# K tiles of four batches, V tiles of two, and extra matmuls in three waits: a change to an attention and MLP decode kernel

## The chip, the cores and the metric

The kernel runs on one core of a Trainium2 chip. A core has TensorE (PE: matmuls, with its weight loads shown apart as PEld), VectorE (DVE), ScalarE (ACT), GpSimd (POOL) and SyncE (SP), and 16 DMA engines that move data between HBM and the on-chip SBUF. Matmuls write to PSUM; DVE and ACT bring results from there to SBUF. The metric is the device time of one execution in microseconds (us), lower is better. Timed without the profiler, the kernel before took 399.53 us (median of three runs, 399.5 to 399.78).

## The reference, cut to what matters

One decode step of a transformer block with adaptive layer norm: 8 batches, one token each, width 512. The attention has 32 query heads over 8 key/value heads (REP = 4), head width 128, and reads the last W = 2048 positions of a cache of 8192. All numbers are 32-bit floats.

```python
mod = (_silu(c) @ w_mod).reshape(c.shape[0], 6, 1, -1)
sa, ca, ga, sb, cb, gb = (mod[:, 0], ..., mod[:, 5])
h = _layernorm(x) * (1 + ca) + sa
# attention: q = h @ wq; k, v = the last W rows of the caches
scores = jnp.einsum("bhqd,bhkd->bhqk", q, k) * (Dh ** -0.5)
p = _softmax(scores, axis=-1)
o = jnp.einsum("bhqk,bhkd->bhqd", p, v)
x = x + ga * (o.reshape(B, Sq, Hq * Dh) @ wo)
h = _layernorm(x) * (1 + cb) + sb
x = x + gb * (relu(h @ w1 + b1) ** 2 @ w2 + b2)
```

The K and the V that are read make 64 MiB each: 8 batches x 8 heads x 2048 x 128 x 4 bytes, twice. The weights add some 30 MB.

## The kernel before, in words

**Tiles.** SBUF holds eight equal buffers, `slots` (L78), of 16 KB per partition, 2 MiB each. Every large load goes into one of them: a K tile (two batches of one key/value head: 64 partitions for each batch, every second partition, 32 positions of 128 numbers on each), a V tile (the same), half of a `wq` group, a `wo` part, parts of `w_mod`, `w1` and `w2`. K and V tiles are loaded by two DMAs of 1 MiB, one for each batch (L97-98).

**Order of the loads.** All of them are issued by SP in one fixed list, `loads` (L132-143): `modA`, two `wq` pieces, then step by step K tile s and V tile s-5, with `wo` parts between, and at the end `modB`, `modC`, the biases, `w1`, `w2`. `pump` (L146) issues the next entries as long as `free` has a buffer; `done` (L151) gives a buffer back when the instruction that last reads it has been written down. The list is strictly in order, so an entry that waits for its buffer holds up all behind it.

**Steps.** The loop at L445 runs 38 steps. N = 32 of them take one K tile each, four (C = 4) for each key/value head. In step s:

- `transposes(s, 0..3)` (L299): 32 PE transposes of 128x128, in eight groups of four into two PSUM buffers; ACT and DVE copy the groups in turn to `kT`. After the last group the K tile is done.
- `scores(s - 1)` (L312): eight products of the padded queries `qpad` with every second column of `kT`, summed into one PSUM tile `s_ps` for the whole head.
- once for each head the softmax in four pieces, `soft_a` to `soft_d` (L328 to L388): copy and maximum, the maximum per query, exponential and sum, transposed probabilities.
- `weighted(s - 5)` (L390): eight products of probabilities with a V tile and four DVE operations that pick the diagonal blocks; then the V tile is done.
- once for each head `gather` (L415) and `project_o` (L431).
- in step 5 `project_q(1)` (L268), which projects the queries of the second half of the heads and ends the use of the last `wq` pieces. `project_q(0)` runs before the loop.

**Tail.** After the loop (L475 on) come the modulation by `modB`, the second layer norm, `h @ w1` (L532: the first two of four row groups, then a wait for the second half of `w1`, then the other two), the DVE work that makes `rT` (L205, L542-544), the bias product (L548), `rT @ w2` in 14 groups of eight instructions (L553), two DVE operations (L561-562) and the store (L563). `w2` arrives in five DMAs: rows 0-4, 4-8, 8-12, 12 and 13 of its 14 groups.

Work between engines is ordered by semaphores; on each engine the instructions run in program order.

Of the kernel before, what the change touches and what calls it, by code (L numbers as in the profile page):

```python
# [14 lines left out]
SLOTS = 8  # L15
V_LAG = 5
PV_LAG = 5
# [3 lines left out]
def tile_adaln_cached_attention_mlp(  # L21
# [34 lines left out]
    ktp = ctx.enter_context(tc.tile_pool(name="ktp", bufs=6))  # L56
# [20 lines left out]

    slots = [consts.tile([P, NJ * DH], F32, name=f"slot{i}") for i in range(SLOTS)]  # L78
    free = list(range(SLOTS))
    held = {}  # L80
    r_kc = "(p kc) n -> p kc n"

    def load(key):
# [5 lines left out]
        s = free.pop(0)  # L89
        t = slots[s]  # L90
        held[key] = s
        if kind in "KV":

            src = k_cache if kind == "K" else v_cache
            hk, c = divmod(i, C)
            v = src[2 * c : 2 * c + 2, hk, SK - W :, :].rearrange("u (p j) d -> u p (j d)", p=H)
            for u in range(2):  # L97
                nc.sync.dma_start(t[u::2, :], v[u])
            return
# [6 lines left out]
        elif kind == "modB":  # L106
            v = w_mod[:, 2 * D : 5 * D].rearrange(r_kc, p=P)[:, 2 * i : 2 * i + 2]
# [5 lines left out]
        elif kind == "w1":  # L113
            v = w1.rearrange(r_kc, p=P)[:, 2 * i : 2 * i + 2]
        else:
            v = w2.rearrange("(p c) n -> p c n", p=P)
            for lo, hi in ((0, 4), (4, 8)) if i == 0 else ((8, 12), (12, 13), (13, 14)):
                o = lo - 8 * i
                n = hi - lo
                nc.sync.dma_start(  # L120
                    t[:, D * o : D * (o + n)].rearrange("p (c n) -> p c n", n=D), v[:, lo:hi, :]
                )
# [4 lines left out]
    def slot(key, n):  # L127

        t = slots[held[key]]
        return t[:, : t.shape[1] // n * n].rearrange("p (a n) -> p a n", n=n)  # L130

    loads = [("modA", 0), ("wq", 0), ("wq", 1)]  # L132
    for s in range(N + V_LAG):
        if s == V_LAG:
            loads += [("wq", 2), ("wq", 3)]
        if s < N:
            loads.append(("K", s))
        v = s - V_LAG
        if v >= 0:
# [3 lines left out]
    loads += [("modB", 0), ("modB", 1), ("modC", 0), ("b", 0), ("w1", 0), ("w1", 1), ("w2", 0), ("w2", 1)]  # L143
    at = [0]

    def pump():  # L146
        while at[0] < len(loads) and (free or loads[at[0]][0] == "b"):
# [3 lines left out]
    def done(*keys):  # L151
        for k in keys:
            free.append(held.pop(k))
# [20 lines left out]
    qpad = consts.tile([P, HKV, B, 32], F32, name="qpad")  # L174
    nc.gpsimd.memset(qpad, 0.0)
# [6 lines left out]
    nc.vector.tensor_reduce(uq, bq.rearrange("p (c u) -> p u c", u=2), axis=AX.X, op=ALU.add)  # L182

# [84 lines left out]
    def project_q(r):  # L268
# [13 lines left out]
        qs = work.tile([P, 512], F32, name="qs", tag="a")  # L282
# [4 lines left out]
        v = pT_.rearrange("p (t g b) -> p g b t", t=REP, g=4)  # L287
        for g in range(4):
            hk = 4 * r + g
            flat = qpad[:, hk].rearrange("p b m -> p (b m)")  # L290
            dest = bass.AP(tensor=flat.tensor, offset=flat.offset, ap=[flat.ap[0], [36, B], [1, REP]])
            nc.vector.tensor_copy(dest, v[:, g, :B, :])
# [6 lines left out]
    def transposes(n, g):  # L299

        k = slot(("K", n), DH)
        t = ktp.tile([P, 8, P], F32, name="kT")
        for a in range(2):
            p = ps_kt.tile([P, 4, P], F32, name="kt_ps")
            for i in range(4):
                nc.tensor.transpose(p[:, i, :], k[:, 8 * g + 4 * a + i, :], ident)  # L306
            (nc.vector.tensor_copy if a else nc.scalar.copy)(t[:, 4 * a : 4 * a + 4, :], p)  # L307
        KTS[n, g] = t
        if g == 3:
            done(("K", n))  # L310

    def scores(n):  # L312
        hk, c = divmod(n, C)
        if c == 0:
            s_ps[0] = ps_1.tile([P, 512], F32, name="s_ps")
        for u in range(2):
            for g in range(4):
                nc.tensor.matmul(  # L318
                    s_ps[0][32 * g : 32 * g + 32, :].rearrange("p (i r) -> p i r", i=8),
                    qpad[:, hk, 2 * c + u, :],  # L320
# [279 lines left out]
```

## Time and profile before

| | |
|---|---|
| time, median of three runs | 399.53 us (399.5 to 399.78) |
| time of the profiled execution | 399.68 us |
| its span, first to last instruction | 397.9 us |
| PE busy | 329.2 us (83%) |
| DVE, ACT busy | 177.1 us (45%), 94.9 us (24%) |
| bytes moved by DMA | 165.25 MB, 415 GB/s over the span |
| granted TensorE clock, mean | 0.979 |

The time of an execution is 1.8 us longer than the span between its first and last instruction. "Busy" counts the time in which an engine works on at least one instruction; PE at 83% is the busiest compute engine. The DMA row gives the mean load of the 16 DMA engines.

### The profile page before, as it was taken

Reading aid. Unit: us, or ns where it says so; the run is one execution under the profiler, and the core shown is the slowest. Engines: PE = TensorE matmul, PEld = TensorE weight load, DVE = VectorE, ACT = ScalarE, POOL = GpSimd, SP = SyncE. Lnnn points to the kernel's source line nnn. Section 1 sums busy time; section 2 is a strip of 40 time slices with the busy share of each in tenths; the row PEclk is TensorE's granted clock in tenths of the full one; section 3 lists DMA queues with packets and bytes.
Section 4 is the critical chain, followed back from the end, with each engine's and each line's share of the span. In section 5 each row is a group of like instructions: output and inputs, shape, how many; then the busy total and the mean of one; then the engine's idle time right before and its main releaser. Section 6 shows DMA issues by size and latency. Waiting matters only on the chain.

```text
span 397.9 us, 6384 instructions
## 1 busy us (share of the span) xinstructions
PE 329.2 (83%) x2632; PEld 168.1 (42%) x2632; DVE 177.1 (45%) x411; ACT 94.9 (24%) x169; POOL 3.3 (1%) x11
## 2 busy tenths in 40 slices
PE   0688889899999999998688899899789998765765
PEld 0245455344454445444344454455344544221124
DVE  6223345344564456445534554456245544542222
ACT  1223244122322322232122232232122312120010
POOL 3000000000000000000000000000000000000000
PEclk9999999999999999999999999999899999998897
DMA  8999999999999999999999999999999999999993
GB/s 308 433 428 423 418 434 423 427 429 418 428 430 428 428 418 432 428 422 425 432 425 427 428 430 424 427 420 430 423 432 425 430 423 431 423 423 417 419 413 128
DMA packets 15357, 165.25 MB, mean 415 GB/s; under 512 B 2392, under 2 KB 2656, under 8 KB 4448
## 3 DMA queue, kind: packets, MB, share of 16 engines
q1 hardware_dynamic: 15184, 164.71, 98.2%
q8 instruction: 21, 0.34, 0.4%
q10 hardware_dynamic: 144, 0.13, 0.1%
q14 instruction: 8, 0.07, 0.0%
HBM read 164.77 MB, written 0.07 MB: 414 GB/s over the span
## 4 chain that ended last, share of the span: by engine, by line
DMA 59%; PE 27%; DVE 8%; ACT 4%; issue 2%; ACTq 0%; DVEq 0%; SPq 0%
DMA slot<-in_A_v_cache_dram 21%; DMA slot<-in_A_k_cache_dram 20%; DMA slot<-in_A_wo_dram 11%; PE kt_ps L306 9%; PE s_ps L318 6%; DMA slot<-in_B_w_dram 5%; PE o_ps L398 4%; DVE kT L307 4%; PE m_ps L273 2%; DMA slot<-in_w_mod_dram 2%; ACT kT L307 2%; DVE o_sb L411 2%; PE m_ps L553 1%; PE m_ps L222 1%; PE m_ps L532 1%
## 5 line engine op out<-in xcount | busy, mean ns | idle before, releaser
L306 PE MATMUL kt_ps<-ident,slot 128*128 128x128 f32 x1024 | 149.2, 283 | 29.1 <-ACT kT L307 13.2
L306 PEld LDWEIGHTS kt_ps<-ident,slot 128*128 128x128 f32 x1024 | 109.6, 142 | 102.7 <-issue 58.2
L307 DVE COPY kT<-kt_ps 128x512 f32<-128x512 f32 x128 | 88.2, 689 | 99.5 <-PE kt_ps L306 86.6
L307 ACT COPY kT<-kt_ps 128x512 f32<-128x512 f32 x128 | 74.8, 584 | 205.6 <-PE kt_ps L306 195.8
L398 PE MATMUL o_ps<-slot,pT 128*32 128x512 f32 x512 | 64.0, 610 | 7.7 <-DMA slot<-in_A_v_cache_dram 6.2
L318 PE MATMUL s_ps<-kT,qpad 128*32 128x512 f32 x512 | 65.4, 627 | 0.0
L411 DVE SCALAR_TENSOR_TENSOR o_sb<-o_ps,diag,o_sb 128x128 f32<-128x128 f32 x96 | 33.7, 351 | 3.4
L409 DVE TENSOR_SCALAR o_sb<-o_ps,diag 128x128 f32<-128x128 f32 x32 | 11.2, 350 | 44.4 <-PE o_ps L398 44.4
L398 PEld LDWEIGHTS o_ps<-slot,pT 128*32 128x32 f32 x512 | 16.4, 110 | 32.7 <-issue 30.3
L318 PEld LDWEIGHTS s_ps<-kT,qpad 128*32 128x32 f32 x512 | 13.5, 109 | 27.2 <-issue 27.2
L222 PE MATMUL m_ps<-slot,cT 128*32 128x256 f32 (+2 forms) x96 | 8.3, 502 | 9.3 <-DMA slot<-in_w_mod_dram 9.3
L332 DVE TENSOR_REDUCE mx<-ss 128x1 f32<-128x512 f32 x8 | 5.5, 686 | 13.7 <-ACT ss L330 13.7
L420 PE MATMUL m_ps<-o_sb,pick 128*32 128x512 f32 x64 | 8.4, 594 | 3.1 <-DVE o_sb L411 1.7
L273 PE MATMUL m_ps<-slot,h1T 128*32 128x512 f32 x64 | 8.9, 703 | 2.0 <-DVE h1T L205 2.0
L378 DVE TENSOR_TENSOR pT<-m_ps,mine 128x512 f32<-128x512 f32 x16 | 10.2, 681 | 0.0
L435 PE MATMUL wo_ps<-slot,oT 128*32 128x512 f32 x64 | 9.3, 651 | 1.1 <-DVE oT L425 1.1
L424 DVE STREAM_TRANSPOSE tr<-m_ps 128x512 f32<-128x512 f32 x8 | 5.7, 716 | 9.5 <-PE m_ps L420 9.5
L222 PEld LDWEIGHTS m_ps<-slot,cT 128*32 128x32 f32 x96 | 3.7, 140 | 13.6 <-issue 13.6
L330 ACT COPY ss<-s_ps 128x512 f32<-128x512 f32 x8 | 4.7, 586 | 18.9 <-PE s_ps L318 18.9
L375 PE MATMUL m_ps<-ident,pr 128*128 128x128 f32 x64 | 8.6, 274 | 0.4 <-DVE pr L359 0.3
L358 ACT ACTIVATE pr<-ss,nm 128x512 f32<-128x512 f32 x8 | 6.2, 774 | 9.7 <-DVE nm L354 9.7
L375 PEld LDWEIGHTS m_ps<-ident,pr 128*128 128x128 f32 x64 | 7.2, 140 | 1.6 <-DVE pr L359 1.2
(114 smaller groups left out, 92.1 us busy)
## 6 DMA issues: line engine op xcount, KB each, us to landing
slot<-in_A_k_cache_dram SPq DMA_DIRECT2D x64, 1024.0 KB, 19.6
slot<-in_A_v_cache_dram SPq DMA_DIRECT2D x64, 1024.0 KB, 19.6
slot<-in_A_wq_dram SPq DMA_DIRECT2D x4, 2048.0 KB, 17.0
slot<-in_A_wo_dram SPq DMA_DIRECT2D x4, 2048.0 KB, 22.0
slot<-in_B_w_dram SPq DMA_DIRECT2D x2, 1792.0 KB, 19.8
slot<-in_w_mod_dram SPq DMA_DIRECT2D x2, 1536.0 KB, 21.4
slot<-in_B_w_dram SPq DMA_DIRECT2D x3, 1024.0 KB, 19.9
slot<-in_w_mod_dram SPq DMA_DIRECT2D x1, 2048.0 KB, 8.4
```

Of the source, the lines that this page charges most:

```text
L222: nc.tensor.matmul(pm[32 * q : 32 * q + 32, : nq * P].rearrange("p (m n) -> p m n", m=nq), cT[:, kc, :], wv[:, :, q, :], start=(kc == 0), ...
L273: nc.tensor.matmul(pq[32 * g : 32 * g + 32, :], hT[:, kc, :], w[:, kc % 2, 512 * g : 512 * g + 512], start=(kc == 0), stop=(kc == NQ - 1),)
L306: nc.tensor.transpose(p[:, i, :], k[:, 8 * g + 4 * a + i, :], ident)
L307: (nc.vector.tensor_copy if a else nc.scalar.copy)(t[:, 4 * a : 4 * a + 4, :], p)
L318: nc.tensor.matmul(s_ps[0][32 * g : 32 * g + 32, :].rearrange("p (i r) -> p i r", i=8), qpad[:, hk, 2 * c + u, :], KTS[n, g][:, :, u::2], ...
L375: nc.tensor.transpose(pp[:, i * P : (i + 1) * P], pr[:, 4 * a + i].rearrange("p r u -> p (r u)"), ident)
L378: nc.vector.tensor_mul(PT_[hk][:, a].rearrange("p x i r -> p i x r"), pp.rearrange("p (i x r) -> p i x r", i=4, r=2 * REP), mine.rearrange ...
L398: nc.tensor.matmul(o[32 * g : 32 * g + 32].rearrange("p j d -> p (j d)"), PT_[hk][:, h, C * g + c].rearrange("p i r -> p (i r)"), v[:, j : ...
L409: nc.vector.tensor_scalar(d, o[:, 0, :], diag[:, 0:1], None, op0=ALU.mult)
L411: nc.vector.scalar_tensor_tensor(d, o[:, j, :], diag[:, j : j + 1], d, op0=ALU.mult, op1=ALU.add)
L420: nc.tensor.matmul(pp[32 * t : 32 * t + 32, :], pick[:, t, :], o.rearrange("p c d -> p (c d)"), start=True, stop=True)
L435: nc.tensor.matmul(wo_ps[32 * i : 32 * i + 32, :], oT[hk % 2][:, i, :], w[:, 4 * (hk % 2) + i, :], start=(hk == 0), stop=(hk == HKV - 1),)
```

## The change

K and V get buffers of their own sizes. Two "big" buffers of 32 KB per partition hold K tiles of four batches (half of the batches of one head), loaded by one DMA of 4 MiB with 32 KB in one piece for each partition; partition 4p + u holds batch u's positions. They hold `modB` and `w1` later. Five "small" buffers of 16 KB hold V tiles (batches c and c + 4, one DMA of 2 MiB each), `wq`, `wo`, `modA`, `modC`, `w2`. The list of loads begins `modA`, two `wq`, K, `wq`, K, `wq`, K. `w2`'s first eight groups come in one DMA.

A K tile is used for two steps. The score product takes every fourth column of `kT`, for four batches, and lands at other rows of `s_ps`: partitions 32u + 8g + 4c + t instead of blocks by g. The zero-padded queries `qpad` are replaced by a window `qwin` of 60 columns with the queries in its middle, copied once for each head by DVE; the place of the window picks the rows. Each call of `scores` now handles one of the four column groups of a K tile, so each step has two calls of four products instead of one call of eight. The softmax index patterns follow the new row order. Several work buffers go from two copies to one, `kT` from six of 4 KB per partition to three of 8 KB.

In the tail, `spin()` is a matmul of the identity with itself (128x512) into a PSUM tile that nobody reads. It stands at three places: before the second half of the `w1` product, before the `w2` loop, and before the twelfth group of that loop.

```diff
-SLOTS = 8
-V_LAG = 5
+K_SLOTS = 2
+V_SLOTS = 5
...
-    ktp = ctx.enter_context(tc.tile_pool(name="ktp", bufs=6))
+    ktp = ctx.enter_context(tc.tile_pool(name="ktp", bufs=3))
...
+    slots = {
+        "big": [consts.tile([P, 2 * NJ * DH], F32, name=f"big{i}") for i in range(K_SLOTS)],
+        "small": [consts.tile([P, NJ * DH], F32, name=f"small{i}") for i in range(V_SLOTS)],
+    }
+    def size_of(key):
+        return "big" if key[0] in ("K", "modB", "w1") else "small"
...
-            src = k_cache if kind == "K" else v_cache
-            hk, c = divmod(i, C)
-            v = src[2 * c : 2 * c + 2, hk, SK - W :, :].rearrange("u (p j) d -> u p (j d)", p=H)
-            for u in range(2):
-                nc.sync.dma_start(t[u::2, :], v[u])
-            return
+            if kind == "K":
+                v = k_cache[4 * (i % 2) : 4 * (i % 2) + 4, i // 2]
+            else:
+                v = v_cache[i % C :: C, i // C]
+            v = v[:, SK - W :, :].rearrange("u (p j) d -> p u (j d)", p=P // v.shape[0])
+            nc.sync.dma_start(t, v)
+            return
...
-            for lo, hi in ((0, 4), (4, 8)) if i == 0 else ((8, 12), (12, 13), (13, 14)):
+            for lo, hi in ((0, 8),) if i == 0 else ((8, 12), (12, 13), (13, 14)):
...
+    loads = [("modA", 0), ("wq", 0), ("wq", 1), ("K", 0), ("wq", 2), ("K", 1), ("wq", 3), ("K", 2)]
+    for q in range(2, N // 2 + 2):
+        if q > 2 and q < N // 2:
+            loads.append(("K", q))
+        for v in (2 * q - 4, 2 * q - 3):
             if v % (2 * C) == 2 * C - 4:
                 loads.append(("wo", v // (2 * C)))
             loads.append(("V", v))
+    loads += [("modB", 0), ("modC", 0), ("b", 0), ("w1", 0), ("w2", 0), ("w2", 1)]
...
+    def scores(q, g):
+        hk, c = divmod(q, 2)
+        if c == 0 and g == 0:
             s_ps[0] = ps_1.tile([P, 512], F32, name="s_ps")
+            nc.vector.tensor_copy(qwin[hk % 2][:, :, 28:32], qall[:, hk])
+        o = 28 - 4 * (2 * g + c)
+        kT = KTS.pop((q, g)).rearrange("p e j (r u) -> p (e j) r u", u=4)
+        for u in range(4):
+            nc.tensor.matmul(
+                s_ps[0][32 * u : 32 * u + 32, :].rearrange("p (i r) -> p i r", i=16),
+                qwin[hk % 2][:, 4 * c + u, o : o + 32],
+                kT[:, :, :, u],
+                start=(c == 0 and g == 0),
+                stop=(c == 1 and g == 3),
+            )
...
     for s in range(N + PV_LAG + 1):
+        q, h = divmod(s, 2)
         if s < N:
-            transposes(s, 0)
+            transposes(q, 2 * h, 0)
...
-            transposes(s, 1)
+            transposes(q, 2 * h, 1)
         if 1 <= s <= N:
-            scores(s - 1)
+            scores((s - 1) // 2, 2 * ((s - 1) % 2) + 1)
...
-            transposes(s, 2)
+            transposes(q, 2 * h + 1, 0)
...
-            transposes(s, 3)
+            transposes(q, 2 * h + 1, 1)
         if i == 0 and 1 <= g <= HKV:
             soft_b(g - 1)
-        if s == V_LAG:
+        if s < N:
+            scores(q, 2 * h)
+        if s == PV_LAG:
             project_q(1)
...
+    spin_ps = ps_kt.tile([P, 4, P], F32, name="kt_ps")
+    def spin():
+        nc.tensor.matmul(spin_ps, ident, ident[:, None, :].to_broadcast([P, 4, P]), start=True, stop=True)
...
             nc.vector.reciprocal(rstd, rstd)
+            spin()
         for g in range(NQ):
...
+    spin()
     for f in range(FC):
+        if f == 12:
+            spin()
         for q in range(NQ):
```

137 lines of the change are left out of this document (67 added, 70 removed).

## The prediction

> **What bounds the kernel now.** I read the page first, for which resource is full all along.
>
> ```profile
> span 397.9 us, 6384 instructions
> DMA  8999999999999999999999999999999999999993
> GB/s 308 433 428 423 418 434 423 427 429 418 428 430 428 428 418 432 428 422 425 432 425 427 428 430 424 427 420 430 423 432 425 430 423 431 423 423 417 419 413 128
> q1 hardware_dynamic: 15184, 164.71, 98.2%
> q8 instruction: 21, 0.34, 0.4%
> ```
>
> The DMA engines are full from the second slice to the last but one, at about 427 GB/s. No compute engine is (PE 83%, in the table above). So the end is set by one stream of 165 MB, if it never runs dry, and by what follows its last byte. SP's own timeline shows the stream's pace, since each issue waits for the transfer eight before it.
>
> ```profile
> 26.54 2.79 SPq L125 DMA_DIRECT2D slot<-in_A_wq_dram  x2
> 32.96 2.89 SPq L98 DMA_DIRECT2D slot<-in_A_k_cache_dram  x2
> ...
> 94.27 2.87 SPq L98 DMA_DIRECT2D slot<-in_A_v_cache_dram  x2
> 99.18 5.39 SPq L98 DMA_DIRECT2D slot<-in_A_k_cache_dram  x2
> ...
> 150.61 2.88 SPq L98 DMA_DIRECT2D slot<-in_A_k_cache_dram  x2
> 155.50 2.88 SPq L98 DMA_DIRECT2D slot<-in_A_v_cache_dram  x2
> ...
> 172.65 2.87 SPq L98 DMA_DIRECT2D slot<-in_A_k_cache_dram  x2
> 179.07 2.89 SPq L98 DMA_DIRECT2D slot<-in_A_v_cache_dram  x2
> ...
> 313.77 7.76 SPq L98 DMA_DIRECT2D slot<-in_A_v_cache_dram  x4
> 325.24 0.37 SPq L125 DMA_DIRECT2D slot<-in_A_wo_dram  x1
> ```
>
> Two DMAs of 1 MiB take 4.89 us (150.61 to 155.50), early and late: never dry. Two things disturb the pace. At 172.65 to 179.07 a pair took 6.42 instead of 4.9, 1.5 us more; so did the pair at 26.54 (6.42), and the four at 313.77 took 11.47 instead of 9.8. The queue that fetches instructions (q8, 21 packets) is the only other traffic then, so I read these as fetches that hit the slowest DMA engine, three of them. And at 99.18 the pair took 5.39 instead of 2.87, because a `wo` DMA of 2 MiB is the one waited for: 2.52 more on a pitch of 2.45, so 4.97 for 2 MiB in 8 KB rows against 4.89 for 2 MiB in 16 KB rows.
>
> Next, whether compute is far behind that pace: the first VectorE operation behind `weighted`, one head (four steps) apart.
>
> ```profile
> 103.61 0.35 DVE L409 TENSOR_SCALAR o_sb<-o_ps,diag 128x128 f32<-128x128 f32 x1 [0.95 <-PE o_ps L398]
> ...
> 143.21 0.35 DVE L409 TENSOR_SCALAR o_sb<-o_ps,diag 128x128 f32<-128x128 f32 x1 [0.95 <-PE o_ps L398]
> ```
>
> Compute needs 39.6 us a head; the stream needs 8 tiles x 4.89 and half a `wo`, 41.6 us. Compute is only 5% faster, so a small loss there would show.
>
> Last, the tail, by the timeline and the windows.
>
> ```profile
> 381.71 1.71 PE L532 MATMUL m_ps<-slot,h2T 128*32 128x448 f32 x16
> 383.35 0.39 PE L527 MATMUL m_ps<-ssb,ones 128*128 128x8 f32 x2
> 385.58 2.69 PE L532 MATMUL m_ps<-slot,h2T 128*32 128x448 f32 x16 [1.84 <-DMA slot<-in_B_w_dram]
> 388.20 0.65 PE L548 MATMUL m_ps<-b_in,ident 4*32 4x128 f32 x8
> 388.32 0.65 DVE L205 STREAM_TRANSPOSE rc<-m_ps 128x448 f32<-128x448 f32 x1 [4.04 <-PE m_ps L532]
> 390.03 4.69 PE L553 MATMUL m_ps<-slot,rT 128*32 128x128 f32 x112 [1.18 <-DVE rT L544]
> 394.80 0.29 DVE L561 TENSOR_TENSOR y<-m_ps,modC 128x128 f32<-128x128 f32 x1 [4.82 <-PE m_ps L553]
> ```
>
> ```profile
> 375.94:379.35 3.41, 2.15 (x32) 0.72 (x24) 1.07 (x5) 0.27 (x1) 0.00 (x0) 1.00 0.98 414
> 382.76:386.18 3.42, 1.58 (x18) 0.58 (x14) 0.20 (x1) 0.27 (x1) 0.00 (x0) 1.00 1.01 417
> 386.18:389.59 3.41, 2.67 (x20) 0.42 (x12) 1.20 (x3) 0.00 (x0) 0.00 (x0) 0.50 0.90 364
> 390.00:393.00 3.00, 2.97 (x56) 2.76 (x60) 0.00 (x0) 0.00 (x0) 0.00 (x0) 0.50 0.44 174
> 393.02:394.75 1.73, 1.70 (x62) 1.40 (x52) 0.00 (x0) 0.00 (x0) 0.00 (x0) 1.00 0.09 30
> 393.60:393.80 0.20, 0.20 (x20) 0.20 (x12) 0.00 (x0) 0.00 (x0) 0.00 (x0) 1.00 0.06 21
> 393.80:394.00 0.20, 0.20 (x17) 0.20 (x8) 0.00 (x0) 0.00 (x0) 0.00 (x0) 1.00 0.00 0
> ```
>
> (The columns are busy time of PE, PEld, DVE, ACT, POOL, then clock, DMA share, GB/s.) The last bytes of `w2` come at about 393.7. PE runs its last stretch at half clock from 386.18 to 393.0, starts 56 of the 112 instructions of L553 in 3.0 us of that, and the last eight only after the bytes: 394.80 is 1.1 us behind them. So two chains end close together, the bytes and PE.
>
> **The change, part by part.** The sum is made on the profiled execution, 399.68 us with a span of 397.9; the median is 399.53, so 0.15 comes off at the end.
>
> *K rows of 32 KB instead of 16.* The stream loses 2048 of K's 4096 row packets, 128 on each of 16 engines. The `wo` comparison prices one: 2 MiB in 8 KB rows is 256 packets, 16 an engine against 8, for 4.97 against 4.89: 0.07 to 0.08 us for 8 more packets, with one completion fewer. That is 9 to 10 ns each if a completion is free, within the few hundredths that such rows are good to; I take 8, the cautious side. 128 x 8 ns = **1.0 us off the stream**. Bounds: nothing, if a row of 32 KB still travels as two packets (no row of the trace is longer than 16 KB); and 2.4, if a completion costs as much as a packet (7 of them for 0.08, 11 ns each), since 82 DMAs go as well (48 of K, 32 of V, one each of `modB` and `w2`). I take 1.0 because one comparison carries it. `w2`'s merged rows add 8 packets x 8 ns, 0.06. V rows stay at 16 KB, the other weights as they are: nothing.
>
> *The buffers: does the stream stay full?* Two K tiles, so tile q+2 can be asked for only when tile q is transposed. Once compute waits for data, tile q has its two steps (20 us) after landing, while 29.4 us of other transfers (four V tiles, one K tile) lie queued; some 2 us go to issue and first bytes: 7 us of slack or more. The beginning is tighter.
>
> ```profile
> 9.30 3.64 PE L222 MATMUL m_ps<-slot,cT 128*32 128x256 f32 x32 [9.30 <-DMA slot<-in_w_mod_dram]
> ```
>
> ```profile
> 24.36 0.45 PE kt_ps L306 x4
> ...
> 25.48 0.67 PE kt_ps L306 x4
> ...
> 39.87 1.94 PE s_ps L318 x16
> ...
> 55.19 1.98 PE s_ps L318 x16
> ...
> 68.84 3.62 PE m_ps L273 x32
> ```
>
> (The second fence is the chain of waits: start, length, what.) `modA` lands at 9.2; at 4.97 for each 2 MiB of weights and 9.8 for each K tile, and 1.5 for a fetch, K0 lands at 29, K1 at 45, `wq` 3 at 50, K2 at 60, V0 to V2 with K3 by 84. K0's two steps of transposes took 24.36 to about 37.2 before (39.87 less the four groups of step 2 at 0.67), 12.8; so K0 is free at 42 and K2 is asked for 7 us ahead. V3 is the tightest: it needs the buffer of `wq` 2, read in `project_q(1)` at step 5, which came 16.3 us after step 4 began (68.84 against 55.19 - 2.7), half of it 1.8 more; from K2's landing at 60 that gives 78, against 82.5. Four microseconds of slack. At the end V30 needs V26's buffer, freed in step 31; about 3. SP is past every such wait in order, so a late entry delays all behind it, but none is late by these numbers. PE starts K0 at 29 instead of 24.4; the slack covers that. Cost: nothing, the cover being these 3 to 7 us.
>
> *The score product.* Same count and shape, a step of four columns instead of two.
>
> ```profile
> L318 PE MATMUL s_ps<-kT,qpad x512: 609/612/1063, 32.4 to 342.6; 128*32 128x512 f32 x171
> L398 PE MATMUL o_ps<-slot,pT x512: 589/592/1061, 73.7 to 368.2; 128*32 128x512 f32 x171
> ```
>
> A step of two costs 612 against 592 ns for adjacent columns, four side by side; by the same law four costs 650, some 0.15 us a step (16 x 40 / 4). Two calls of half the size leave ACT and DVE shorter pauses, some gain. Once a head the product waits for the new copy to `qwin`, behind `soft_b`'s two DVE operations and the last `kT` copy: about 1.2 us in which PE, `weighted` queued behind, stands. Less the shorter pauses, 39.6 becomes 40 to 41 a head, still under 41.6: nothing on the path. Bounds: -0.5 to +2 us a step, the second end being a product that takes twice its time. Single work buffers: each is read to its end a step before it is written again, nothing. Softmax with other strides, one copy for four in `project_q`: some tenths on engines at 24 and 45%, hidden by the same slack.
>
> *The spins.* One is a full product of 512 columns; the nearest row, eight score products in two rounds of four in 1.94 us (the chain of waits, above), gives 0.97, at half clock (53 against 28 ns, below) 1.8. The first lies between 383.7 and the arrival of `w1` at 385.54, hidden. A window of 3.41 us with PE busy 2.15 kept the clock, one with 1.58 lost it; 1.58 + 0.95 = 2.53 keeps it. Then L532 takes 1.71 instead of 2.69, `rT` is there 1.0 earlier at about 389.05, the second spin lies before that, L553 goes at 28 ns an instruction (62 in 1.73) instead of 53, and the twelve groups are done by 391.8, the third spin by 392.7, when the last bytes still come until 393.6. Groups 12 and 13 then end about 0.5 behind them instead of 1.1: **0.7 us off** (0.6 to 0.75), if the clock stays.
>
> By the Trainium skill ("TensorE: Matmul & The Clock Gate", section "Why this matters for your kernels") only idle gaps above some 3 us drop the clock; the longest gap here is 1.84, so by that rule the spins gain nothing and the sum would be 0.7 higher. The trace speaks against it: the window from 382.76 has no longer gap and is followed by 0.50.
>
> Sum: span 397.9 - 1.06 - 0.7 = 396.1; time 399.53 - 1.8 = **397.7**.
>
> **Rivals.**
>
> *Packets stay at 16 KB.* The transfers then do nothing new; the spins alone give 399.53 - 0.7 = 398.8. For: no row longer than 16 KB in the trace. Against: the page's 15184 packets on q1 are just one for each row that the kernel's loads and store name (12808) and one completion for each engine of each DMA (148 x 16 + 8), so rows up to 16 KB are not cut. 0.12.
>
> *Fetches fall otherwise.* Three of 21 hit the slowest engine at 1.5 us each. Same PE instruction count but for 12, so probably the same places; one fewer gives 396.2, one more 399.2. 0.07 each.
>
> *Compute becomes the bound (slower).* Place: the score product and the `qwin` wait. Price: from 0.5 us a step on, 39.6 + 1.2 + 2.0 = 42.8 a head passes 41.6 by enough to use up the 7 us within six heads; then K tiles are asked for late and SP holds all. At 1 us a step: 44.8, 3.2 a head over; after two heads five more lose it, 16 us: 414. For: only 5% between the two paces. Against: the 20 ns that a step of two cost. 0.12, most of it nearer 401.
>
> *K's rows come slower (slower).* One DMA now steps through four batches 32 MiB apart, 32 KB each; before, each DMA read one unbroken 1 MiB. K is 16 x 9.8 = 157 us of the stream, so each percent costs 1.6 us, and 1.1% eats the gain; at 4%, 404. Nothing in the trace reads so far apart. 0.06.
>
> [...]
>
> *The clock drops all the same.* Half clock from 386.18 as before: the bias product ends at 388.85, the second spin at 390.65, 44 instructions of L553 start by 393.0, the other 52 of the twelve groups at 28 ns end at 394.5, the third spin at 395.4, the last 16 with their latency at 396.1: 1.3 later than before, less the stream's 1.06 gives 399.8; about 402 if the clock does not come back at 393. 0.03 and 0.02.
>
> **How the numbers follow.** Forecast 0.51, its own range 396.4 to 398.4 (the bounds of packets and spins). The measurement tells about 0.2%, 0.8 us, from no change: faster is below 398.7. Faster: 0.51 + 0.07 for one fetch fewer, less 0.02 for a late buffer that costs a microsecond: 0.56. Same: packets 0.12, one more fetch 0.07, clock 0.03, that 0.02: 0.24. Slower: compute 0.12, K's rows 0.06, clock 0.02: 0.20. For eight in ten the range runs from 395.9 (one fetch fewer) to 401.5 (the near part of compute, the clock, K slower by 2%); beyond it lie some 0.15, the far ends of compute and of K's rows.
>
> **What would show it.** Right: 11696 packets on q1 (2048 rows of K, 128 of `w2` and 82 x 16 completions fewer), slices still at 9, a K tile's pitch of 9.7 us instead of 9.79; PE waiting for K tiles and SP for DMAs, not the other way round; after `w1` lands, clock 1.00 and L532 at 1.7. Wrong: slices of DMA under 9 in the middle, SP waiting for PE at K or V3; the same packet count; L318 far above 650 ns; K issues more than 9.9 us apart while DMA is full.

## The result, and the profile after

| | before | after |
|---|---|---|
| time, median of four runs | 399.57 us (399.5 to 399.78) | 453.94 us (453.66 to 454.32) |
| ratio | | 1.1363 (95% interval 1.1348 to 1.1377) |
| profiled execution, its span | 399.68, 397.9 us | 454.32, 452.5 us |
| PE busy | 329.2 us | 386.4 us |

The kernel became 54.4 us slower. The first place to look is the row that was full before. From the page of the kernel after:

```profile
span 452.5 us, 6171 instructions
...
DMA  8999999399999898699989896999979883949993
GB/s 322 443 426 413 434 422 424 122 440 414 448 408 439 345 403 340 267 431 428 417 306 416 327 405 245 379 437 433 384 319 377 366 348 136 369 185 389 418 427 151
...
q1 hardware_dynamic: 11696, 164.71, 88.3%
...
PE 64%; DVE 14%; DMA 11%; ACT 7%; issue 2%; SPq 0%; ACTq 0%; DVEq 0%
...
L340 PE MATMUL s_ps<-kT,qwin 128*32 128x512 f32 x512 | 127.1, 1072 | 7.9 <-DVE qwin L336 7.9
```

The DMA engines run dry again and again: slices at 122, 136, 185 and 245 GB/s where all between the ends stood near 427. The chain of work that ended last is now mostly PE's (64%; before it was DMA 59%, PE 27%), and in it is a group that has nearly doubled: the 512 instructions of the score product are busy for 127.1 us, 1072 ns each, four of them side by side. What SP waited for tells where the stream can be held (line, releaser, sum in us, times, longest), first before, then after:

```profile
SPq L98 <- DMA slot<-in_A_k_cache_dram: 120.2, 62, 3.6
```

```profile
SPq L106 <- PE kt_ps L326: 297.3, 36, 16.5
...
SPq L106 <- PE m_ps L293: 23.7, 1, 23.7
```

Before, SP waited for transfers; now 297.3 us of its waiting ends with a transpose of PE, and 23.7 us once with `project_q(1)`, the wait of V3, in front of the first dry slice (122). The 297.3 us alone do not show that PE holds the stream: the fastest kernel below, whose stream is full, has 268.5 us of the same wait, since there too SP issues a large K tile and then stands until PE has freed the next buffer. It is the dry slices together with the wait that show it. The compute side's own pace stands in DVE's timeline, by the first operation behind `weighted`, one head apart:

```profile
127.95 0.35 DVE L442 TENSOR_SCALAR o_sb<-o_ps,diag 128x128 f32<-128x128 f32 x1 [3.83 <-PE o_ps L431]
...
176.25 0.35 DVE L442 TENSOR_SCALAR o_sb<-o_ps,diag 128x128 f32<-128x128 f32 x1 [3.83 <-PE o_ps L431]
...
224.55 0.35 DVE L442 TENSOR_SCALAR o_sb<-o_ps,diag 128x128 f32<-128x128 f32 x1 [3.83 <-PE o_ps L431]
```

A head takes 48.3 us, where compute took 39.6 before and the stream 41.6. The parts add up: the product's busy time grew from 65.4 to 127.1 us, 7.7 a head (its group on the page before is the first row below), and once a head it stands behind the copy to `qwin` (the second fence, PE's timeline of the kernel after):

```profile
L318 PE MATMUL s_ps<-kT,qpad 128*32 128x512 f32 x512 | 65.4, 627 | 0.0
```

```profile
220.78 1.99 PE L340 MATMUL s_ps<-kT,qwin 128*32 128x512 f32 x8 [1.00 <-DVE qwin L336]
```

39.6 + 7.7 + 1.0 = 48.3. Against the stream's 41.6 that is 6.7 us too much in each of eight heads, 54 us, about the whole loss. That it comes out so exactly is in part chance: the same reckoning for the kernel before with a step of four (below) gives 42 us where 34 were measured, so some 8 us are absorbed there. The kernel after begins its transposes 4.7 us later than the kernel before (28.9 against 24.2), which eats into such a lead. What had to be found out is why its instruction takes 1072 ns, and what the other parts of the change are worth when it doesn't.

### The profile page after: what moved, and what is told of

Read it like the earlier page. It is cut to its first block, busy times and chain, and to the rows that moved or that the text cites. A ratio compares the mean times of both kernels' runs of the same rounds, so it can differ in the third digit from the quotient of the medians.

```text
span 452.5 us, 6171 instructions
## 1 busy us (share of the span) xinstructions
PE 386.4 (85%) x2638; PEld 167.4 (37%) x2638; DVE 176.6 (39%) x416; ACT 97.6 (22%) x169; POOL 2.5 (1%) x12
## 3 DMA queue, kind: packets, MB, share of 16 engines
q1 hardware_dynamic: 11696, 164.71, 88.3%
## 4 chain that ended last, share of the span: by engine, by line
PE 64%; DVE 14%; DMA 11%; ACT 7%; issue 2%; SPq 0%; ACTq 0%; DVEq 0%
PE s_ps L340 27%; PE kt_ps L326 20%; PE o_ps L431 12%; DMA big<-in_A_k_cache_dram 6%; DVE kT L327 6%; ACT kT L327 5%; DMA small<-in_B_w_dram 5%; DVE o_sb L444 3%; PE wo_ps L468 1%; PE m_ps L453 1%; DVE o_sb L442 1%; DVE mx L352 1%; DVE pT L411 1%; ACT ss L350 1%; PE m_ps L293 1%
## 5 line engine op out<-in xcount | busy, mean ns | idle before, releaser
L326 PE MATMUL kt_ps<-ident,big 128*128 128x128 f32 x1024 | 150.8, 285 | 27.2 <-ACT kT L327 18.8
L326 PEld LDWEIGHTS kt_ps<-ident,big 128*128 128x128 f32 x1024 | 110.7, 143 | 130.2 <-issue 77.8
L340 PE MATMUL s_ps<-kT,qwin 128*32 128x512 f32 x512 | 127.1, 1072 | 7.9 <-DVE qwin L336 7.9
L431 PE MATMUL o_ps<-small,pT 128*32 128x512 f32 x512 | 61.3, 596 | 0.0
L431 PEld LDWEIGHTS o_ps<-small,pT 128*32 128x32 f32 x512 | 17.6, 117 | 59.8 <-issue 59.1
L340 PEld LDWEIGHTS s_ps<-kT,qwin 128*32 128x32 f32 x512 | 10.2, 108 | 19.9 <-DVE qwin L336 10.2
L242 PE MATMUL m_ps<-small,cT 128*32 128x256 f32 (+1 forms) x64 | 4.5, 444 | 9.3 <-DMA small<-in_w_mod_dram 9.3
L384 ACT ACTIVATE pr<-ss,nm 128x512 f32<-128x512 f32 x8 | 9.7, 1208 | 11.1 <-DVE nm L381 11.1
L293 PE MATMUL m_ps<-small,h1T 128*32 128x512 f32 x64 | 9.9, 777 | 2.2 <-DVE h1T L225 2.2
L468 PE MATMUL wo_ps<-small,oT 128*32 128x512 f32 x64 | 8.4, 594 | 1.1 <-DVE oT L458 1.1
## 6 DMA issues: line engine op xcount, KB each, us to landing
small<-in_B_w_dram SPq DMA_DIRECT2D x1, 2048.0 KB, 23.1
```

What stands on the lines that cost most here:

```text
L293: nc.tensor.matmul(pq[32 * g : 32 * g + 32, :], hT[:, kc, :], w[:, kc % 2, 512 * g : 512 * g + 512], start=(kc == 0), stop=(kc == NQ - 1),)
L326: nc.tensor.transpose(p[:, i, :], k[:, 32 * e + 8 * g + 4 * a + i, :], ident)
L340: nc.tensor.matmul(s_ps[0][32 * u : 32 * u + 32, :].rearrange("p (i r) -> p i r", i=16), qwin[hk % 2][:, 4 * c + u, o : o + 32], kT[:, :, ...
L431: nc.tensor.matmul(o[32 * g : 32 * g + 32].rearrange("p j d -> p (j d)"), PT_[hk][:, h, 4 * c + g].rearrange("p i r -> p (i r)"), v[:, j : ...
L468: nc.tensor.matmul(wo_ps[32 * i : 32 * i + 32, :], oT[hk % 2][:, i, :], w[:, 4 * (hk % 2) + i, :], start=(hk == 0), stop=(hk == HKV - 1),)
```

## The experiments

### Is it the columns, the buffers, or the rows?

Three things changed around the product at once: the step of its columns, buffers four times as coarse for K, and rows of 32 KB. Three kernels part them.

**Adjacent columns, all else of the change kept:**

```diff
-        kT = KTS.pop((q, g)).rearrange("p e j (r u) -> p (e j) r u", u=4)
+        kT = KTS.pop((q, g)).rearrange("p e j (u r) -> p (e j) r u", u=4)
```

> The changed kernel with one index changed: each score product reads 32 adjacent columns (32u to 32u+31 of each block of 128) in place of every fourth; so the scores pair queries with positions of the wrong batches, all counts and shapes stay. Theory S (the step of four makes the product slow, compute becomes the bound, buffers come free late): the product's instructions fall from 1072 to about 600 ns, its busy time from 127 to about 65 us, the DMA slices are 9 throughout, time 397 to 401. Rival B (two coarse K buffers starve the stream whatever the product costs): the product is fast but SP still waits for PE at K tiles, time above 430. Rival R (K's rows from four batches are read slowly): time above 410 with the DMA engines full and K tiles more than 9.9 us apart.

Measured: 400.59 us (median of 10, 399.87 to 401.32), before 399.49, ratio 1.0027 (1.0018 to 1.0037). The rows of that line in the kernel with adjacent columns (shortest, median, longest in ns; first and last start):

```profile
L340 PE MATMUL s_ps<-kT,qwin x512: 592/593/617, 36.6 to 351.3; 128*32 128x512 f32 x171
```

One edit of the access takes back some 53.3 of the 54.4 us. Buffers, rows and order of loads do not make the loss by themselves.

**The kernel before, with a step of four alone:**

```diff
-                    KTS[n, g][:, :, u::2],
+                    KTS[n, g].rearrange("p j (r m) -> p j m r", m=4)[:, :, 2 * u : 2 * u + 2, :],
```

> The kernel before, with the score product reading its 64 columns of each block as two runs of 32 with a step of four (the other positions than every second; scores go to wrong batches). Buffers, DMAs, counts as before. Theory S: 1070 ns an instruction instead of 612, 1.9 us a step more, compute 39.6 + 7.7 = 47.3 us a head against the stream's 41.6; 8 heads at 5.7 less what the buffers absorb (about 8 us): 432 to 445. Rivals B and R: this kernel has neither the coarse buffers nor the far rows, so 399 to 401.

Measured: 433.34 us (433.05 to 434.91, 4 runs), ratio 1.0854 (1.0834 to 1.0875). From its rows of that line, and DVE's timeline:

```profile
L318 PE MATMUL s_ps<-kT,qpad x512: 1059/1078/1146, 32.5 to 389.4; 128*32 128x512 f32 x171
```

```profile
152.90 0.35 DVE L409 TENSOR_SCALAR o_sb<-o_ps,diag 128x128 f32<-128x128 f32 x1 [1.13 <-PE o_ps L398]
...
199.69 0.35 DVE L409 TENSOR_SCALAR o_sb<-o_ps,diag 128x128 f32<-128x128 f32 x1 [1.12 <-PE o_ps L398]
```

The step alone makes an instruction 1078 ns long and the kernel 34 us slower, without a 32 KB row or a big buffer. A head takes 46.8 us here against 48.3 in the kernel after; the 1.5 more (1.0 of it the `qwin` wait) make 12 of the 20.6 us between the two kernels. The two profiles part the rest: the transposes begin 4.5 us later in the kernel after (28.9 against 24.4 us), and from the last of these DVE operations to the end of the span it takes 28.4 us (424.14 to 452.5) instead of 23.1 (408.23 to 431.3).

**Seven other steps, one in each head of the kernel before** (one execution, 410.49 us):

```diff
+                if hk == 0:
+                    nc.tensor.matmul(o3, qv, kt[:, :, u::2], start=st, stop=sp)
+                elif hk == 1:
+                    nc.tensor.matmul(o3, qv, kt[:, :, 64 * u : 64 * u + 64], start=st, stop=sp)
+                elif hk == 2:
+                    k3 = kt[:, :, :96].rearrange("p j (r m) -> p j m r", m=3)[:, :, u : u + 2, :]
...
+                elif hk == 6:
+                    kp = kt.rearrange("p j (r m) -> p j r m", m=4)[:, :, :, 2 * u : 2 * u + 2]
...
```

> The kernel before with another step of the score product in each head, always 512 columns: steps of 2, 1, 3, 4, 8, 16 columns, then pairs of adjacent columns at a step of 4, then a step of 5 (scores of wrong positions in all heads but the first). If the cost comes from the span of memory that the columns reach over, it rises with the step: 612, 592, about 840, 1072, 2100, 4200, and pairs like 4. If each access brings a small group of adjacent columns of which a step of four or more uses one, it is flat from 4 on: about 592, 612, 830 at 3, 1072 at 4, 5, 8 and 16, and pairs at 4 like a step of 2. The total is not the point of this run.

The instructions of the tile `s_ps`, one line of the program for each head; in this order the steps are 2, 1, 3, 4, 8, 16, then pairs of adjacent columns every four, then 5:

```profile
L325 PE MATMUL s_ps<-kT,qpad x64: 609/612/638, 33.4 to 57.6; 128*32 128x512 f32 x64
L327 PE MATMUL s_ps<-kT,qpad x64: 592/592/617, 63.7 to 99.1; 128*32 128x512 f32 x64
L330 PE MATMUL s_ps<-kT,qpad x64: 845/852/869, 107.2 to 142.1; 128*32 128x512 f32 x64
L333 PE MATMUL s_ps<-kT,qpad x64: 1064/1078/1082, 150.5 to 188.6; 128*32 128x512 f32 x64
L336 PE MATMUL s_ps<-kT,qpad x64: 1081/1097/1100, 197.2 to 235.6; 128*32 128x512 f32 x64
L339 PE MATMUL s_ps<-kT,qpad x64: 1025/1038/1083, 244.2 to 282.2; 128*32 128x512 f32 x64
L342 PE MATMUL s_ps<-kT,qpad x64: 609/612/637, 290.8 to 322.3; 128*32 128x512 f32 x64
L345 PE MATMUL s_ps<-kT,qpad x64: 1094/1117/1139, 330.4 to 366.1; 128*32 128x512 f32 x64
```

The price is neither a straight line nor a matter of distance. It is almost flat from 1 to 2, climbs from 2 to 4, and is flat again up to 16. Pairs spread over the same distance as a step of four cost what a step of two costs. The number of dimensions of the access is not it either: the pairs have three and cost 612, the kernel after has two and costs 1072. What these cases share is how many of the columns read lie in one group of four columns, 16 bytes: four, two, one and a third, one. At one column to a group, 512 columns take 1078 ns, 2.1 ns a group; at one and a third, 384 groups take 852, 2.2 ns each; at two, 256 groups would need about 550 and are hidden behind the pace of the columns, 592 ns. That a group is what one access brings is my reading of eight durations; the durations are measured.

### The same scores without a step

**A permuted identity in the transposes.** The transpose is a matmul with an identity. If the identity's columns are sorted by batch, `kT` comes out with each batch's positions side by side, and the product reads adjacent columns, all of its own batch. Relative to the kernel after:

```diff
+    identp = consts.tile([P, P], F32, name="identp")
+    nc.vector.tensor_copy(identp.rearrange("p (u r) -> p u r", u=4), ident.rearrange("p (r u) -> p u r", u=4))
...
-                nc.tensor.transpose(p[:, i, :], k[:, 32 * e + 8 * g + 4 * a + i, :], ident)
+                nc.tensor.transpose(p[:, i, :], k[:, 32 * e + 8 * g + 4 * a + i, :], identp)
...
-        kT = KTS.pop((q, g)).rearrange("p e j (r u) -> p (e j) r u", u=4)
+        kT = KTS.pop((q, g)).rearrange("p e j (u r) -> p (e j) r u", u=4)
```

> The changed kernel with the transposes' identity replaced by a permuted one, so that the columns of one batch come out side by side in kT (for each u the 32 columns 4r+u) and the product reads adjacent columns; the numbers computed are those of the changed kernel. Theory S: the same time as e1, 397 to 401, product about 600 ns. If the transposes do not follow the permutation, the time is the same and the scores are of other positions. Rivals B and R: above 410 as in e1.

Measured: 400.85 us (399.15 to 402.41, 10 runs), ratio 1.0031 (1.0016 to 1.0046). So this is the change with the score product at the price that I had forecast, or a little under it (604 ns on its page), and it is still no gain. The sort itself is free: the transposes have a median of 273 ns with either identity. DVE's timeline gives its pace:

```profile
125.25 0.35 DVE L444 TENSOR_SCALAR o_sb<-o_ps,diag 128x128 f32<-128x128 f32 x1 [2.05 <-PE o_ps L433]
...
166.18 0.35 DVE L444 TENSOR_SCALAR o_sb<-o_ps,diag 128x128 f32<-128x128 f32 x1 [2.06 <-PE o_ps L433]
```

40.9 us a head, under the stream's 41.6: the steps are not the bound any more. What is left lies in the tail and in short dry spots. Its timeline of the tail:

```profile
387.94 0.28 DVE L589 SCALAR_TENSOR_TENSOR rT<-relu 128x112 f32<-128x112 f32 x1
...
389.77 4.47 PE L601 MATMUL m_ps<-small,rT 128*32 128x128 f32 x96 [1.86 <-DMA small<-in_B_w_dram]
...
394.17 1.12 PE L518 MATMUL kt_ps<-ident 128*128 128x512 f32 x2
...
395.22 0.65 PE L601 MATMUL m_ps<-small,rT 128*32 128x128 f32 x16
```

`rT` is ready at 388.2, but the merged `w2` piece of eight groups is not there until 389.8, so PE stands for 1.86 us. Then the 96 instructions take 4.47 us (47 ns each, near the half-clock price of 53; the granted clock from 389.7 to 394.2 is 0.62), the third spin starts at 394.17, and the last two groups wait for it until 395.22. Each of these was taken away in turn.

### The tail, one edit at a time

**Without the third spin**, relative to the kernel with the permuted identity:

```diff
-        if f == 12:
-            spin()
```

> The permuted kernel (e4) without the third spin, the one before the twelfth group of the w2 loop. Theory T (in e4 the third spin stands on the path: PE ends the twelve groups at 394.2, runs the spin until 395.2 and only then the last groups, whose bytes landed at 393.4): the last groups follow at once, 1.05 us less than e4: 399.8. Rival H (the spin is hidden behind the last bytes, as the prediction had it): the same as e4, 400.9.

Measured: 399.26 us (398.37 to 399.9, 10 runs), before 399.39, ratio 0.9994 (0.9984 to 1.0004). Against before the kernel moved from +1.36 to -0.13 us, 1.5 by the medians. Of this 1.05 us is the spin itself, by the rows above. The rest need not be the spin's: in the profiled execution of this kernel the granted clock was 1.00 in the `w2` loop, and its first 64 instructions took 1.96 us, 31 ns each, ahead of the place where the spin had stood.

```profile
389.73 1.96 PE L599 MATMUL m_ps<-small,rT 128*32 128x128 f32 x64 [1.52 <-DMA small<-in_B_w_dram]
```

**Also `w2` in the old pieces:**

```diff
-            for lo, hi in ((0, 8),) if i == 0 else ((8, 12), (12, 13), (13, 14)):
+            for lo, hi in ((0, 4), (4, 8)) if i == 0 else ((8, 12), (12, 13), (13, 14)):
```

> e5 with the first eight groups of w2 again in two DMAs of 1 MiB. Theory T: in e4 rT is there at 388.2, but the merged DMA lands only at 389.6; PE stands idle, loses the clock for a window and starts 1.6 us late. With two pieces the first groups run from 388.3 at full clock, and PE follows the pieces as they land; the end is about 0.5 us behind the last of them: 2.0 under e4, 398.9 (a stream about 0.8 shorter than before, a tail as before). Rival H: the start of the loop does not matter, 399.8 as e5.

Measured: 399.10 us (398.57 to 399.66, 10 runs), ratio 0.9994 (0.9985 to 1.0004). 0.16 us less than without the split, within the spread of either kernel.

**Also without the other two spins:**

```diff
-            spin()
...
-    spin()
```

> e6 without any spin. If the spins keep the clock up in the waits and that matters, L532's successor takes about 2.7 us instead of 1.7, the w2 loop runs at half clock as in the kernel before, and the time is 0.1 to 0.7 over e6. If the end follows the last bytes either way, it is within 0.2 of e6.

Measured: 399.42 us (398.44 to 400.56, 10 runs), ratio 0.9998 (0.9988 to 1.0009), not to be told from the two above. The timelines say why. With both spins (the kernel with `w2` split):

```profile
380.41 1.71 PE L577 MATMUL m_ps<-big,h2T 128*32 128x448 f32 x16 [0.23 <-DMA big<-in_B_w_dram]
...
392.07 1.75 PE L599 MATMUL m_ps<-small,rT 128*32 128x128 f32 x48 [1.43 <-DMA small<-in_B_w_dram]
```

and without any:

```profile
380.71 3.22 PE L576 MATMUL m_ps<-big,h2T 128*32 128x448 f32 x16
...
392.38 1.76 PE L597 MATMUL m_ps<-small,rT 128*32 128x128 f32 x48 [1.41 <-DMA small<-in_B_w_dram]
```

The clock does differ early in the tail: the first half of the `w1` product takes 3.22 us instead of 1.71. The spins are not the reason, since it lies ahead of them, and in the kernel with two spins and merged `w2` it takes 3.06. But in both kernels the last six groups of `w2` start when their bytes come, after 1.4 us of idle PE, and take the same 1.75. A PE that is faster before that point only waits longer.

**The kernel before with all three spins, and with the first two alone** (the second without the last two lines):

```diff
             nc.vector.reciprocal(rstd, rstd)
+            spin()
...
+    spin()
     for f in range(FC):
+        if f == 12:
+            spin()
```

> The kernel before with the three spins at the three places and nothing else. As the prediction had it: 0.7 us faster, 398.8. By theory T: in the kernel before the piece of groups 8 to 11 lands at about 392.9, their matmuls end at 393.8, the spin at 394.8, the last groups at 395.3, where they ended at 394.8 without: 0 to 0.6 slower, 399.5 to 400.1.

> The kernel before with the first two spins only. Theory T: the third spin made all of the 0.84 us that the three spins cost (400.23); without it the last groups follow the bytes, 1.05 less than that: 399.2, within 0.3 of the kernel before. The prediction's 0.7 off would be 398.7.

Measured: three spins 400.23 us (400.12 to 400.42, 10 runs), ratio 1.0021 (1.0012 to 1.0031); two spins 399.43 (399.17 to 400.65, 11 runs), ratio 0.9995 (0.9984 to 1.0005). The first two bring nothing that can be told from the spread, and the third costs 0.8 to 0.9. In the timeline of the kernel with three:

```profile
385.56 1.71 PE L538 MATMUL m_ps<-slot,h2T 128*32 128x448 f32 x16
...
389.05 2.19 PE L562 MATMUL m_ps<-slot,rT 128*32 128x128 f32 x64 [0.37 <-DVE rT L550]
392.63 1.08 PE L562 MATMUL m_ps<-slot,rT 128*32 128x128 f32 x32 [1.39 <-DMA slot<-in_B_w_dram]
393.65 1.12 PE L478 MATMUL kt_ps<-ident 128*128 128x512 f32 x2
394.70 0.65 PE L562 MATMUL m_ps<-slot,rT 128*32 128x128 f32 x16
```

The clock is kept, as the second half of the `w1` product shows (1.71 us; 2.69 before), but groups 8 to 11 wait for their bytes until 392.63. They end at 393.71; the last two start a microsecond later, for the spin between them. (It stands in front of the group with number 12, counted from 0, so of the last two.) In the profiled execution of the kernel with two, the slowest of its 11 at 400.65, the last 48 instructions, behind two waits for bytes (idle gaps of 1.02 and 1.40 us), run at a granted clock of 0.50:

```profile
392.93 2.79 PE L560 MATMUL m_ps<-slot,rT 128*32 128x128 f32 x48 [1.40 <-DMA slot<-in_B_w_dram]
```

### The rows of 32 KB

**K back in rows of 16 KB, in the kernel with `w2` split:**

```diff
-            nc.sync.dma_start(t, v)
+            if kind == "K":
+                half = NJ * DH
+                nc.sync.dma_start(t[:, :half], v[:, :, :half])
+                nc.sync.dma_start(t[:, half:], v[:, :, half:])
```

> e6 with each K tile loaded by two DMAs of 16 KB rows in place of one with 32 KB rows: 2048 packets and 16 DMAs more, nothing else. If a row packet costs 8 ns as the prediction had it, K tiles come 9.79 us apart again instead of 9.72 and the stream is 1.1 us longer: 400.2 against 399.1 of e6. Rival: the 32 KB rows bring nothing, 399.1.

Measured: 400.18 us (399.32 to 400.57, 11 runs), ratio 1.0009 (0.9999 to 1.002), against 0.9994 with 32 KB rows. By the medians, each against its own runs of before, the long rows gain 1.0 us (+0.68 against -0.29); by the ratios 0.6. The two intervals overlap a little (0.9999 to 1.002 and 0.9985 to 1.0004), so the sign is likely and the size is good to half a microsecond. The run changes a little more than the rows: there are 16 DMAs more, and the halves of a tile are asked for one after the other (SP issues them at 40.55 and 42.05 us for K2).

### The tight buffers

The kernel with `w2` split keeps a dry spot near the end. Its windows (busy time of PE, PEld, DVE, ACT, POOL, then clock, DMA share, GB/s):

```profile
340.00:350.00 10.00, 8.76 (x76) 4.40 (x72) 4.08 (x8) 2.34 (x4) 0.00 (x0) 1.00 1.02 432
350.00:360.00 10.00, 6.31 (x56) 2.38 (x44) 5.64 (x17) 3.33 (x5) 0.00 (x0) 1.00 0.87 349
```

83 GB/s less for 10 us is 0.83 MB, 1.9 us at 432 GB/s by this count. The prediction had named two buffers with little slack, those of V3 and V30.

**V3's alone: `project_q(1)` earlier, so that `wq`'s buffer is free for it:**

```diff
-        if s == PV_LAG:
+        if s == 3:
             project_q(1)
```

> e6 with project_q(1) in step 3 instead of step 5, so that the buffers of wq pieces 2 and 3 come free earlier. In e6 the transfer of V3 starts late (the first engine's pitch there is 5.5 us in place of 4.9, SP waiting 20 us for project_q). Theory D (the stream runs dry at V3 and costs 0.4 us there): 0.4 less than e6, 398.7, SP's wait for project_q gone. Rival: the engines catch up at the second dry place (V30), the time stays 399.1.

Measured: 399.46 us (398.65 to 400.59, 10 runs), ratio 0.9996 (0.9985 to 1.0008). No gain. Its window of the late dry spot:

```profile
350.00:360.00 10.00, 6.40 (x50) 2.80 (x43) 5.56 (x17) 3.34 (x5) 0.00 (x0) 0.92 0.89 336
```

**V30's too: it goes into a K buffer, which is idle by then:**

```diff
-        return "big" if key[0] in ("K", "modB", "w1") else "small"
+        return "big" if key[0] in ("K", "modB", "w1") or key == ("V", 30) else "small"
...
-            nc.sync.dma_start(t, v)
+            nc.sync.dma_start(t if kind == "K" else t[:, : NJ * DH], v)
```

> e10 with V tile 30 in a 32 KB buffer (the one that K tile 14 left), so that V30 and V31 need not wait for weighted of tiles 25 and 26. In e6 the slices at 350 to 360 us move 349 GB/s. Theory D: the slice goes back to about 425, some 0.8 us less than e10: 397.9 to 398.3, 0.3% under the kernel before. Rival: the slowest DMA engine was not dry there, only the others, and the time stays that of e10.

Measured: 398.44 us (398.07 to 398.76, 5 runs), before 399.5, ratio 0.9968 (0.9956 to 0.9981). The same window, and the tail in PE's timeline:

```profile
350.00:360.00 10.00, 6.38 (x51) 2.69 (x44) 5.76 (x17) 3.34 (x5) 0.00 (x0) 0.94 1.00 423
```

```profile
391.49 1.71 PE L599 MATMUL m_ps<-small,rT 128*32 128x128 f32 x48 [1.45 <-DMA small<-in_B_w_dram]
```

The dry spot is gone, and the bytes that the last six groups of `w2` wait for are there 0.6 us earlier than in the kernel with `w2` split (391.49 against 392.07). This kernel, the change with the permuted identity, two spins, `w2` in the old pieces, `project_q(1)` earlier and V30 in a K buffer, is faster than both kernels of the case: by 0.3% than before. Its page and SP's wait:

```profile
span 396.4 us, 6166 instructions
...
DMA  8999999999999999999999999999999999999993
...
DMA packets 12011, 165.22 MB, mean 417 GB/s; under 512 B 1096, under 2 KB 1360, under 8 KB 3152
```

```profile
SPq L108 <- PE kt_ps L328: 268.5, 35, 19.9
```

The stream is full from end to end again, with 32 KB rows. Whether V30's buffer would do it without the earlier `project_q(1)` was not tried.

## Why the prediction was wrong, by its own steps

The forecast was 397.7 us with a range up to 401.5; the time is 453.94.

**The score product, the step that failed.** "A step of two costs 612 against 592 ns for adjacent columns, four side by side; by the same law four costs 650, some 0.15 us a step." It costs 1073, and some 1.9 us a step. There was no law: two points, by the reading above both in the range where the pace of the columns hides the accesses, were extended past the place where it stops hiding them. The upper bound of the same paragraph, "a product that takes twice its time", is what happened, and the rival built on it has the right place and mechanism. By its own rule, two us a step and the 1.2 for `qwin` give 48.8 a head, 7.2 over the stream; one head to use up the 7 us of slack and seven more make 50 us, 450. Its chance was 0.12, "most of it nearer 401", argued from those same 20 ns, and the end of the range followed that chance instead of the bound. Twenty nanoseconds at one step were taken as evidence on another that no row showed.

**The `qwin` wait: right.** 1.2 forecast, 1.00 measured on the product's row.

**The pace of compute without that step: right.** "40 to 41 a head" forecast, 40.9 in the kernel with the permuted identity. The "shorter pauses" that this had counted as a gain do not show: 39.6, the 1.0 of the `qwin` wait and 0.35 of a product that is busy for 68.2 us in place of 65.4 make 40.95. That K0's later start costs nothing holds there too; with the slow product the same start is part of the loss.

**Softmax with other strides: right in effect.** Its exponential was one of the operations counted as "some tenths", hidden. It took 774 ns (the page before):

```profile
L358 ACT ACTIVATE pr<-ss,nm 128x512 f32<-128x512 f32 x8 | 6.2, 774 | 9.7 <-DVE nm L354 9.7
```

and takes 1208, 0.43 us a head more (the page after):

```profile
L384 ACT ACTIVATE pr<-ss,nm 128x512 f32<-128x512 f32 x8 | 9.7, 1208 | 11.1 <-DVE nm L381 11.1
```

**K's rows of 32 KB: right.** 11696 packets on q1, as forecast, so the rival in which packets stay at 16 KB falls. Put back, the short rows cost 0.6 to 1.0 us where 1.0 was forecast. The rival in which K comes more slowly falls too: with V30's buffer freed, the stream of 32 KB rows is full in every slice and moves 417 GB/s over the span, against 415 before. These rows come from four batches 32 MiB apart, and the rate is that of before. The 9.7 us between K tiles that the prediction names as a sign cannot be read off SP's issues here, since SP waits for PE and not for a transfer. For the same reason SP waiting for PE at K was no good sign of being wrong: the fastest kernel shows it too (268.5 us).

**The slack of the buffers: named rightly, sized too large.** "Four microseconds" for V3 and "about 3" for V30, "none is late by these numbers". V3, reckoned to be asked for at 78, is asked for at 79.8 us in the kernel with `w2` split and at 88.1 in the kernel after. V30 was late by enough to leave a dry spot of 1.9 us by its bytes; freeing its buffer was worth 1.0 us (399.46 to 398.44), and both edits together, each kernel against its own runs of before, 0.8 (-0.29 to -1.06). Where the rest of the 1.9 went is open.

**The spins: wrong.** "0.7 us off", with the third spin hidden because the twelve groups would be done by 391.8. Groups 8 to 11 get their bytes only at about 392.6, so the third spin starts at 393.65 and stands before the last two groups: 0.8 to 0.9 us in the kernel before, at least 1.05 in the change. Also an instruction of the loop takes 34 ns at full clock there (64 in 2.19 us), not 28. The first two keep the clock up as forecast as far as the loop (the second half of the `w1` product takes 1.71 instead of 2.69 us), but what they gain ends in a wait for bytes. With groups 8 to 11 there at 392.63 and the last 48 instructions in some 1.7 us, the loop would end at about 394.3 (an estimate from these rows), 0.4 before the 394.72 of the kernel before, and the runs do not show even that. The step had read "the last bytes" from the DMA share, which tells when the transfers end, and not when each piece may be used.

**`w2`'s merged rows: wrong in kind.** Counted at 0.06 gained for fewer packets, while the merged piece holds back the first four groups until the second four are there: the 1.86 us of idle PE in the tail. Splitting it again was worth 0.16 us, not to be told from nothing, since the bytes behind it set the end.

**The clock.** That it drops all the same was a rival at 0.05. In the `w2` loop it did in two kernels with spins: with the permuted identity, where 96 instructions ran at 47 ns each behind a gap of 1.86 us, and in the kernel before with two spins, where 48 ran at 58 ns each behind one of 1.40. It did not in the kernel without the third spin, behind a gap of 1.52 us. So the length of the last gap does not decide it, and what does was not worked out. The Trainium skill's rule ("TensorE: Matmul & The Clock Gate", section "Why this matters for your kernels") that only gaps above some 3 us count, cited in the prediction, does not fit this either: the gaps are 1.86 and 1.40 us.

**The fetches.** 20 packets on q8 after, in place of 21; a stream that is not full shows nothing of what one of them costs. The kernel before with three and with two spins has a full stream and 21 packets; there the pairs that took 6.42 us take 6.10 and 5.67 (at 26 us) and 6.01 and 5.54 (at 172), and the four at 313 take 9.79 and 9.78, no delay at all; with two spins others come late instead (5.84 at 83.6, 5.67 at 229.7). So a fixed 1.5 us for each of three fetches does not hold; what makes the delays stays open.

Put together, with the product repaired, of the forecast's two gains the one for rows is about right (0.6 to 1.0 of 1.06 us) and the 0.7 for spins became a loss. The best kernel stands 1.06 us under the runs of before (399.5 to 398.44). That this is the forecast's figure for rows is chance: it is the sum of several edits that the change does not have.

## What to carry to other kernels

A duration measured at steps of one and two says nothing about a step of four: where a change leaves the range that the trace shows and the bound at the other end is a factor of two on the busiest engine, time that one instruction first, or give the bound its weight. Where a layout asks for a stepped operand and its producer is a transpose by an identity, permute the identity: the sort was free here. And extra matmuls that keep the clock up brought nothing where the bytes set the end; ahead of the last pieces of a stream they are themselves the tail.

## What the runs showed of the hardware that was not expected

The moving operand of a matmul in 32-bit floats, four products side by side, costs 592, 612, 852 and 1078 ns for 512 columns at steps of 1, 2, 3 and 4, then 1117, 1097 and 1038 at 5, 8 and 16; pairs of adjacent columns at a step of four cost 612. The Trainium skill ("SBUF — State Buffer", section "Door 1: The DMA port swizzle (why `[64,N]` ≈ `[32,N]`)") says that SBUF has lines of 16 bytes and that two accesses to a line are needed for full bandwidth. The runs agree: two columns to a line (a step of two, or pairs) are nearly free, one and a third and one are not. The same place gives four 32-bit numbers as the step that is free; here four costs 1078 against 592, and the measurement decides: two is free, four is not.

The exponential on ACT shows the same direction for stepped writes, 774 ns with every second column and 1208 with every fourth; its reads are in order in both kernels. Whether the step of the writes or the longer access pattern makes the difference was not tried.
